# P V groups in any order, a slot for every x row, GpSimd scaling in quarters, the last two softmax blocks scaled on chip: one change to a fused attention and ReGLU kernel

## The chip, the cores and the metric

The kernel runs on one core of a Trainium2 chip. The metric is the device time in microseconds (us). The time before was given as 798.48 us, median of three runs. Every experiment was run beside the kernel before on the same chip; those runs of the kernel before lie between 796.4 and 802.4 us. Medians of different calls therefore differ by up to 1.8 us for the same kernel; the ratios are free of that. All profiles used here were at a mean granted TensorE clock of 0.987 to 1.0. PE is TensorE, ACT is ScalarE, DVE is VectorE, POOL is GpSimd, SP is the engine that issues transfers.

## The reference

2048 rows of width 512 in bf16, 32 heads of 16, hidden width 1792.

```python
xn = layernorm(x)
q, k, v = split(xn @ wqkv)                       # 32 heads of 16
p = softmax(q @ k.T / 4);  o = p @ v             # per head, 2048 keys
h = relu(xn @ W_gate) * (xn @ W_up)
return x + o @ wo + h @ W_down
```

## The kernel before

The kernel is written as a graph of operations. A list scheduler in Python, with an assumed length and latency for each operation, puts them into one queue per engine, and each queue runs in order on the chip. An operation with `lock=True` is kept apart, in the scheduler's own clock, from locked operations of the other engine of the pair GpSimd and DVE. Constants steer it.

```python
PV_LAG = 4.0; D_TAIL = 4; D_LEAD = 10.0; K_ACT = (1, 2)
O_LAST = 66; O_BEG = 22; EV = -940.0; PACE_L = 1.0; KEEP = 4.0; RIDE = 40.0
LAT = {"PE": 150.0, "ACT": 220.0, "DVE": 100.0, "POOL": 120.0, "SP": 0.0}
```

The scores of a unit (128 keys by 512 queries of one head) are computed on PE into PSUM. ACT exponentiates most of them into a ring of six slots; 98 groups of four are exponentiated on DVE by bit operations (four passes out of PSUM, then four long instructions in SBUF, the last two with two inputs). PE multiplies the exponentials by V ("P V"), accumulating in one PSUM bank; column 16 of V is ones, so the row sums come with it. PE fills its spare time with the GLU and with matmuls on zeros.

The parts that the change touches (cuts marked):

```python
# 1 the ones of v_aug: after the fourth row's normalisation in program order only
G.op("POOL", 2500, lambda e: e.memset(v_aug[:, :, :, DH:VN], 1.0), ..., order=t_xn0)
# 2 16 row blocks of x share two slots of four
P_x = Pool("x", 2);  t_x = [Tile("x", P_x) for _ in range(NB)]
# 3 a finished block: sums to DRAM, reciprocal on GpSimd, broadcast back, then one scaling
G.op("POOL", 1280, lambda e: e.tensor_tensor(oT_of(tn), o_sb[:, to.slot, :], rb[:, trb.slot, :], ALU.mult), ..., lock=True)
# 4 P V writes its bank strictly in the order of the units
G.op("PE", 225, pv, mode="col", reads=rd, writes=[pv_tile[key]], prio=u + PV_LAG, ...)
# 5 the very last block on chip: 16 columns of sums, reciprocal, spread by matmuls, product
ins = e.matmul(ps_b[:, 2, 4 * c:4 * c + 4], src(128 * c, 128 * c + 128), ident32[:, DH:128:32], ...)
G.op("DVE", 200, lambda e: e.reciprocal(rrec2[:], ps_b[:, 2, 0:16]), ...)
...  # spread: 16 matmuls of rrec2 columns against the identity; then one product of 128x512
```

The softmax here doesn't subtract the row's maximum and nothing guards it: scores larger than these inputs give would overflow.

Of the kernel before, what the change touches and what calls it, by code (L numbers as in the profile page):

```python
# [6 lines left out]
FP32 = mybir.dt.float32  # L7
# [4 lines left out]
ALU = mybir.AluOpType  # L12
# [16 lines left out]
NRING = 6  # L29
PV_LAG = 4.0  # L30
PV_MIN = 2
# [5 lines left out]
D_SKIP = 14  # L37
D_TAIL = 4
D_LEAD = 10.0
D_WAIT = 1.0  # L40

XT_ACT = ((1,), ())
K_ACT = (1, 2)
V_ACT = (0, 1, 2, 4)
N_POOL = ()
HX = 4
O_END = 70
O_LAST = 66
O_BEG = 22
EV = -940.0  # L50
PACE_L = 1.0

# [33 lines left out]
class Graph:  # L86
# [4 lines left out]
    SWITCH = 100.0  # L91
    KEEP = 4.0
    RIDE = 40.0
    WINDOW = 3400.0
# [51 lines left out]
    def run(self):  # L146
# [111 lines left out]
        self.held = {"DVE": 0.0, "POOL": 0.0}  # L258
        total = len(ops)
        while n < total:  # L260
            best = None
            for e in self.ENGS:
                pick = None
                for o in cand[e]:
                    at = earliest(o)
                    if at is None:
                        continue
                    same = o.mode is not None and o.mode == mode[e]
                    ready = free[e] + (0.0 if same or o.mode is None or mode[e] is None else self.SWITCH)
                    at = max(at, ready)  # L270
                    if o.lock:
                        at = max(at, self.held["POOL" if e == "DVE" else "DVE"])
                    late = at > ready + 1e-6
                    key = (late, at if late else 0.0, o.prio - (self.KEEP if same else 0.0), o.idx)
                    if pick is None or key < pick[0]:
                        pick = (key, at, o)
                if pick is not None and (best is None or pick[1] < best[0]):
                    best = (pick[1], e, pick[2])
            if best is None:
                raise AssertionError("no operation can be placed: %s" % [  # L280
                    (o.name, o.eng) for e in self.ENGS for o in cand[e]][:12])
            at, e, o = best
            if e == "PE":
                if self.fill is not None:
                    blanks(at, o)
                ran.append((at, at + o.dur))
# [125 lines left out]
def bass_parallel_sum__mha_block__glu_gated_reglu__prompt_kernel(  # L412
# [16 lines left out]
    with ExitStack() as es:  # L429
# [40 lines left out]
        ident32 = sb("ident32", [128, 128], FP32)  # L470
        rrec2 = sb("rrec2", [128, 16], FP32)
        ps_sc = es.enter_context(nc.psum_tensor("ps_sc", [128, 5, 512], FP32))
# [15 lines left out]
        P_oT = Pool("oT", 9)  # L488
        P_x = Pool("x", 2)
        P_xr = Pool("xr", 2)  # L490
# [42 lines left out]
        for i in range(2):  # L533
            dma(lambda e, i=i: e.dma_start(q_scr[i, :, DH:2 * DH, :], qT[:, 0, :]), 128,
                reads=[t_qt0], writes=[t_qz[i]], prio=-600)
        t_x = [Tile("x", P_x) for _ in range(NB)]
        t_xm = [Tile() for _ in range(NT)]

        def xs(m):
            return x_sb[:, 4 * t_x[m // 4].slot + m % 4, :]  # L540

        def load_x(m0, n, prio):
            t = t_x[m0 // 4]
            dma(lambda e: e.dma_start(x_sb[:, 4 * t.slot + m0 % 4:4 * t.slot + m0 % 4 + n, :], x_src[:, m0:m0 + n, :]), 128 * n,
                writes=([t] if m0 % 4 == 0 else []), prio=prio)
            o = G.ops[-1]
            if m0 % 4:
                t.r.append(o)
                o.order.add(t.w[0])
            for m in range(m0, m0 + n):  # L550
                t_xm[m].w.append(o)
# [14 lines left out]
        load_x(8, 4, -894)  # L566
        load_x(12, 4, -893)
        dma(lambda e: e.dma_start(Wk[:, :, 128:512], w_src[:, :, D + 128:2 * D]), 384, writes=t_wk[1:], prio=-892)
# [282 lines left out]
        ln_block(0, -800)  # L851
        G.op("POOL", 2500, lambda e: e.memset(v_aug[:, :, :, DH:VN], 1.0), writes=[t_vones], prio=-500, order=t_xn0)
        proj_q(0, 0, -790, tile=t_pro[0], sub=1, eng="ACT")
# [14 lines left out]
        guard = Tile("x")  # L868
        for t in t_x[2:]:
            guard.r.extend(t.w + t.r)  # L870
        P_oT.cur[0:8] = [guard] * 8

        def oT_of(t):
# [127 lines left out]
        t_os, o_last = {}, [[], []]  # L1001

        def last_normalise(to, pr):
            def src(a=0, b=512):
                return o_sb[:, to.slot, a:b]

            t_s, t_r, t_b = Tile("ls", P_b, [2]), Tile(), Tile("lb", P_sc, [1])

            def sums(e):
                ins = None  # L1010
                for c in range(4):
                    ins = e.matmul(ps_b[:, 2, 4 * c:4 * c + 4], src(128 * c, 128 * c + 128), ident32[:, DH:128:32], start=True, stop=True)
                return ins
            o = G.op("PE", 900, sums, mode="full", reads=[to, t_id32], writes=[t_s], prio=pr - 100)
            o.opens = ("tail", [o])
            G.op("DVE", 200, lambda e: e.reciprocal(rrec2[:], ps_b[:, 2, 0:16]), reads=[t_s], writes=[t_r], prio=pr - 900)

            def spread(e):
                ins = None
                for c in range(4):  # L1020
                    for j in range(4):
                        ins = e.matmul(ps_sc[32 * j:32 * j + 32, 3, 128 * c:128 * c + 128],
                                       rrec2[:, 4 * c + j:4 * c + j + 1].to_broadcast([128, 32]), ident32[:],
                                       start=True, stop=True, tile_position=(0, 32 * j))
                return ins
            G.op("PE", 900, spread, mode="col", reads=[t_r, t_id32], writes=[t_b], prio=pr - 100).opens = ()
            tn = Tile("oT", P_oT)
            G.op("DVE", 610, lambda e: e.tensor_tensor(oT_of(tn), ps_sc[:, 3, :], src(), ALU.mult),
                 reads=[t_b, to], writes=[tn], prio=pr - 900)
            return tn  # L1030

        def normalise(c4, gg, ee):
# [3 lines left out]
            to = Tile("o", P_o)  # L1036
            G.op("DVE", 610, lambda e: e.tensor_copy(o_sb[:, to.slot, :], ps_b[:, 0, :]), reads=[tp], writes=[to], prio=-950, name="oev%d" % n)  # L1037
            pr = upos(c4, gg, ee, NT) + 1
            if (c4, gg, ee) == (NB - 1, NGG - 1, 1):
                t_oT[(c4, NGG + ee)] = last_normalise(to, pr)  # L1040
                return
            ts, trr, tsc, trb = Tile("rs"), Tile("rr"), Tile("sc"), Tile("rb", P_rb)
            par = n % 2
            if n >= 2:
# [10 lines left out]
            tn = Tile("oT", P_oT)  # L1055
            G.op("POOL", 1280, lambda e: e.tensor_tensor(oT_of(tn), o_sb[:, to.slot, :], rb[:, trb.slot, :], ALU.mult),  # L1056
                 reads=[to, trb], writes=[tn], prio=pr, lock=True)
            if (c4, gg) == (NB - 1, NGG - 1):
                t_oT[(c4, NGG + ee)] = tn
                return  # L1060
            par = gg % 2
# [12 lines left out]
        def pv_group(key, kt, u):  # L1074
# [12 lines left out]
            for k in range(3 if on else 1):  # L1087
                def pv(e, k=k):
                    ins = None
                    for j in range(4):  # L1090
# [3 lines left out]
                    return ins  # L1094
                G.op("PE", 225, pv, mode="col", reads=rd, writes=[pv_tile[key]], prio=u + PV_LAG, name="pv%d" % u,
                     after=u + PV_MIN)
                if first and k == 0:
                    G.ops[-1].opens = ("pv", [G.ops[-1]])
# [90 lines left out]

        lead = None  # L1190
        for i in range(4):
            tz = Tile("fin", P_sc if i == 0 else P_b if i == 3 else None, [0] if i == 0 else [1])
            if i < 3:
                tz.bank = i
            n0 = len(G.ops)
            m = 12 + i
            if i >= 2:
                G.op("PE", 900, lambda e, i=i, tz=tz: e.matmul(bank_of(tz), ident32[:], resid(i), start=True, stop=False),
                     mode="full", reads=[t_id32, t_res[m]], writes=[tz], prio=NU - 20 if i == 3 else NU + 2)
            for g, pr in ((2, NU - 10), (4, NU - 9), (5, NU + 10)):  # L1200
                to = t_oT[(3, g)]

                def fn(e, i=i, g=g, to=to, tz=tz):
                    ins = None
                    for j in range(4):
                        ins = e.matmul(bank_of(tz)[32 * j:32 * j + 32, :], oT_of(to)[:, 128 * i + 32 * j:128 * i + 32 * j + 32],
                                       Wo[:, g, :] if g < NGG else Wo_p[:, g - NGG, :],
                                       start=(g == 2 and i < 2), stop=(g == 5), tile_position=(0, 32 * j))
                    return ins
                G.op("PE", 216, fn, mode="col", reads=[to, t_wo, t_wop], writes=[tz], prio=pr + (i if g == 5 else 0.1 * i if i < 3 else -9))  # L1210
            mm = [o for o in G.ops[n0:] if o.eng == "PE"]
            if lead is None:
                lead = mm[0]
            elif i < 3:
                for o in mm:
                    o.order.add(lead)
            to_ = Tile("ost", P_xn)
            if i < 2:
                G.op("DVE", 610, lambda e, i=i, to_=to_, tz=tz: e.tensor_tensor(xn_sb[:, to_.slot, :], bank_of(tz), resid(i), ALU.add),
# [55 lines left out]
```

## Time and profile before

| stretch of the kernel before | us |
|---|---|
| start to first exponential | 13.86 |
| first to last exponential | 772.9, of which ACT busy 760.6, idle 12.3 |
| after the last exponential ("tail") | 10.65 |
| span of the profiled run | 797.4 |

### The profile page before, as it was taken

What the parts mean: (1) busy time and instruction counts of PE and PEld (TensorE: products, weight loads), DVE (VectorE), ACT (ScalarE), POOL (GpSimd) and SP (SyncE); (2) the same over time, 40 slices, a digit from 0 to 9 for tenths busy, and PEclk for the clock granted to TensorE, in tenths of its full rate; (3) what the DMA queues carried; (4) which work ended last, traced back from release to release, by engine and by line L of the source; (5) the groups of instructions that cost most, each with busy time, mean ns of one, the idle gap of its engine ahead of it and who ended that gap; (6) DMA issues with size and microseconds to landing.
All of it is one profiled execution on the core that took longest, in us unless ns stands there. A gap on an engine that the chain in (4) does not pass through costs nothing.

```text
span 797.4 us, 21196 instructions
## 1 busy us (share of the span) xinstructions
PE 763.8 (96%) x9386; PEld 226.4 (28%) x9386; DVE 746.9 (94%) x1060; ACT 765.7 (96%) x679; POOL 159.1 (20%) x90
## 2 busy tenths in 40 slices
PE   7999999999999999999999999999999999999997
PEld 3322222222222232222222322222222222222322
DVE  7769999999999999999999999999999999999983
ACT  5899999999999999999999999999999999999995
POOL 3101222211221201223121122121122211122111
PEclk9999999999999999999999999999999999999999
DMA  5132121212121121221222112221222113222001
GB/s 175 50 117 79 34 69 50 55 48 55 49 67 50 28 80 49 68 62 35 61 58 67 35 43 74 58 58 41 73 50 69 41 40 82 62 70 71 21 24 42
DMA packets 96163, 47.10 MB, mean 59 GB/s; under 512 B 70216, under 2 KB 92104, under 8 KB 96072
## 3 DMA queue, kind: packets, MB, share of 16 engines
q1 hardware_dynamic: 96072, 45.74, 21.2%
q8 instruction: 74, 1.21, 0.7%
q14 instruction: 17, 0.14, 0.1%
HBM read 36.96 MB, written 8.51 MB: 57 GB/s over the span
## 4 chain that ended last, share of the span: by engine, by line
DVE 49%; PE 40%; ACT 9%; issue 1%; POOL 0%; DMA 0%; ACTq 0%
DVE dring L1127 16%; PE ps_b L682 15%; PE ps_sc L1111 11%; PE ps_b L1092 9%; ACT ring L1179 9%; DVE dring L1143 8%; DVE dring L1144 8%; DVE dring L1139 4%; DVE dring L1141 4%; PE ps_b L1111 3%; DVE up_sb L898 3%; DVE hT L902 2%; DVE Wv L1037 1%; PE ps_b L1230 1%; DVE qT L737 1%
## 5 line engine op out<-in xcount | busy, mean ns | idle before, releaser
L1179 ACT ACTIVATE ring<-ps_sc 128x1536 bf16<-128x1536 f32 (+1 forms) x663 | 757.3, 1277 | 10.4 <-PE ps_sc L1111 5.6
L1127 DVE TENSOR_SCALAR dring<-ps_b 128x512 uint16<-128x512 f32 x392 | 268.9, 686 | 18.0 <-PE ps_b L1111 15.4
L1111 PE MATMUL ps_sc<-qm,kT 32*128 32x512 bf16 x1656 | 264.2, 385 | 5.9 <-ACT ring L1179 3.7
L1048 POOL TENSOR_TENSOR rrec<-rsum,minus 128x16 f32<-128x16 f32 x31 | 100.9, 3255 | 386.0 <-DMA rsum<-Wv 386.0
L1111 PE MATMUL ps_b<-qm,kT 32*128 32x512 bf16 x392 | 150.0, 383 | 9.7 <-DVE dring L1127 8.3
L1092 PE MATMUL ps_b<-ring,v_aug 128*17 128x512 bf16 x1656 | 149.4, 382 | 1.8 <-DVE Wv L1037 1.7
L1111 PEld LDWEIGHTS ps_sc<-qm,kT 32*128 32x128 bf16 x1656 | 63.4, 91 | 234.2 <-ACT ring L1179 194.6
L1143 DVE TENSOR_TENSOR dring<-dring 128x2048 f16<-128x2048 bf16 x98 | 123.2, 1257 | 0.0
L1144 DVE TENSOR_TENSOR dring<-dring 128x2048 bf16<-128x2048 bf16 x98 | 122.4, 1249 | 0.1
L1056 POOL TENSOR_TENSOR x_sb<-Wv,rb 128x512 bf16<-128x512 f32 x26 | 38.2, 1469 | 175.8 <-DMA rb<-rec_scr 175.8
L1139 DVE TENSOR_SCALAR dring<-dring 128x2048 uint16<-128x2048 uint16 x98 | 69.5, 710 | 1.3
L1141 DVE TENSOR_SCALAR dring<-dring 128x2048 uint16<-128x2048 uint16 x98 | 69.9, 713 | 0.0
L682 PE MATMUL ps_b<-xnT,wgs 128*32 128x512 bf16 x896 | 68.1, 384 | 1.3 <-DVE up_sb L898 1.1
L682 PE MATMUL ps_b<-xnT,wus 128*32 128x512 bf16 x896 | 67.5, 384 | 1.6 <-DVE qT L737 0.6
L1092 PE MATMUL ps_b<-dring,vd 128*17 128x512 bf16 x784 | 66.6, 381 | 0.0
L682 PE MATMUL ps_b<-Wd,hT 128*32 128x512 bf16 x768 | 59.7, 383 | 0.0
L1092 PEld LDWEIGHTS ps_b<-ring,v_aug 128*17 128x17 bf16 x1656 | 37.4, 89 | 65.3 <-issue 45.8
L1111 PEld LDWEIGHTS ps_b<-qm,kT 32*128 32x128 bf16 x392 | 35.6, 91 | 64.3 <-DVE dring L1127 48.3
L1230 PE MATMUL ps_b<-zeros 128*17 128x512 bf16 x560 | 47.4, 382 | 0.0
L1092 PE MATMUL ps_b<-dring,v_aug 128*17 128x512 bf16 x392 | 38.4, 382 | 3.1 <-DVE dring L1144 1.6
L898 DVE COPY up_sb<-ps_b 128x512 f32<-128x512 f32 x56 | 38.3, 684 | 0.8 <-PE ps_b L682 0.7
L902 DVE SCALAR_TENSOR_TENSOR hT<-ps_b,up_sb 128x512 bf16<-128x512 f32 x48 | 32.9, 684 | 0.6 <-PE ps_b L682 0.6
(99 smaller groups left out, 357.8 us busy)
## 6 DMA issues: line engine op xcount, KB each, us to landing
rb<-rec_scr SPq DMA_DIRECT2D x31, 256.0 KB
wus<-in_B_W_up_dram SPq DMA_DIRECT2D x56, 128.0 KB, 3.1
wgs<-in_B_W_gate_dram SPq DMA_DIRECT2D x56, 128.0 KB, 2.4
qm<-q_scr SPq DMA_DIRECT2D x30, 128.0 KB
o_scr<-x_sb SPq DMA_DIRECT2D x25, 128.0 KB
q_scr<-qT SPq DMA_DIRECT2D x17, 128.0 KB
xr_sb<-in_A_x_dram SPq DMA_DIRECT2D x16, 128.0 KB, 3.3
out_dram<-xn_sb SPq DMA_DIRECT2D x16, 128.0 KB, 1.7
```

The lines of the kernel that those rows point to most:

```text
L682: ins = e.matmul(bank_of(tile, sub)[32 * j:32 * j + 32, :], st[:, 32 * j:32 * j + 32], mv, start=(i == 0), stop=(i == n - 1), tile_positio ...
L898: G.op("DVE", 610, lambda e: e.tensor_copy(up_sb[:, tup.slot, :], bank_of(tu)), reads=[tu], writes=[tup], prio=slots[1] + EV)
L1048: G.op("POOL", 3000, lambda e: e.tensor_tensor(rrec[:, par, :], rsum[:, par, :], minus[:, 0:1].to_broadcast([128, 16]), ALU.pow), reads=[t ...
L1092: ins = e.matmul(ps_b[32 * j:32 * j + VN, 0, :], v, src[j][1](k), start=(first and k == 0), stop=(last and (k == 2 or not on)), tile_posit ...
L1111: return e.matmul(bank, kT[32 * j:32 * j + 32, gg, 128 * kt:128 * kt + 128], qm[32 * j:32 * j + 32, t_q[(c4, gg)].slot, ee, :], start=True ...
L1127: o = G.op("DVE", 610, lambda e, j=j: e.tensor_scalar(dring[:, tr.slot, 0, 512 * j:512 * j + 512].bitcast(U16), ps_b[:, 2, :], 0.25 * LOG2 ...
L1139: G.op("DVE", 600, lambda e: e.tensor_scalar(b(2, U16), b(0, U16), 0x7F, 0x3F80, op0=ALU.bitwise_and, op1=ALU.bitwise_or), reads=[tr], wri ...
L1141: G.op("DVE", 600, lambda e: e.tensor_scalar(b(1, U16), b(0, U16), 0xFF80, N_MANT, op0=ALU.bitwise_and, op1=ALU.bitwise_or), reads=[tr], w ...
L1143: G.op("DVE", 1140, lambda e: e.tensor_tensor(b(2, FP16), b(2), b(2), ALU.mult), reads=[tm], writes=[tm], prio=u - 3, name="d4", lock=True)
L1144: G.op("DVE", 1140, lambda e: e.tensor_tensor(b(2), b(0), b(2, FP16), ALU.mult), reads=[tm, tr], writes=[tm], prio=u - 3, name="d5", lock= ...
L1179: return e.activation(ring[:, a:a + n, :], ps_sc[:, 3 * k0:3 * k0 + n, :], ACTF.Exp, scale=0.25)
L1230: ins = e.matmul(ps_b[32 * j:32 * j + VN, 0, :], zeros[:, 0:VN], zmov, start=False, stop=False, tile_position=(0, 32 * j))
```

## The change

Its intent: remove the collisions between GpSimd and DVE, keep ACT fed when a third block of keys is due and when a DVE group is late, and shorten the end.

```diff
-        G.op("POOL", 2500, ...memset..., prio=-500, order=t_xn0)
+        G.op("POOL", 2500, ...memset..., prio=-500, lock=True)      # now waits for the normalisations
+        for o in t_xn0: G.ops[-1].deps[o] = True
-            return x_sb[:, 4 * t_x[m // 4].slot + m % 4, :]
+            return x_sb[:, m, :] if m < 8 else hT[:, m - 8, :]      # a slot for every x row
-            G.op("POOL", 1280, ...tensor_tensor of 128x512...)
+            for k in range(N_MUL): ...  # four of 128x128, name="pm"
+                    if o.name == "pm" ...:  # scheduler: start a quarter with DVE's newest instruction,
+                        ...                 # if that one takes no lock and is long enough
+                if PV_FREE and not (first and k == 0): ...  # P V after the first in any order
-            G.op("DVE", 200, lambda e: e.reciprocal(rrec2[:], ps_b[:, 2, 0:16]), ...)
+            # last block in two halves: sums broadcast to all rows by matmuls, then
+            G.op("DVE", 400, lambda e, h=h, bank=bank: e.reciprocal(rb[..256 columns..], bank()), ...)
+            # the block before it, too, leaves the DRAM trip and is scaled on chip:
+            G.op("DVE", 680, lambda e: e.reciprocal(rb[:, tr.slot, :], ps_b[:, 1, :]), ...)
-PV_LAG = 4.0  D_TAIL = 4  D_LEAD = 10.0  O_LAST = 66  O_BEG = 22  EV = -940.0  PACE_L = 1.0  KEEP = 4.0  RIDE = 40.0
+PV_LAG = 3.0  D_TAIL = 6  D_LEAD = 9.0   O_LAST = 74  O_BEG = 20  EV = -12.0   PACE_L = 0.9  KEEP = 8.0  RIDE = 20.0
...  # K_ACT = (1, 2, 3); the last units' P V given priority; the order of the last output matmuls; one residual added on PE instead of two
```

## The prediction

> **What bounds the kernel now.** I began with the page: busy shares, then the costliest groups.
>
> ```profile
> PE 763.8 (96%) x9386; PEld 226.4 (28%) x9386; DVE 746.9 (94%) x1060; ACT 765.7 (96%) x679; POOL 159.1 (20%) x90
> L1179 ACT ACTIVATE ring<-ps_sc 128x1536 bf16<-128x1536 f32 (+1 forms) x663 | 757.3, 1277 | 10.4 <-PE ps_sc L1111 5.6
> L1230 PE MATMUL ps_b<-zeros 128*17 128x512 bf16 x560 | 47.4, 382 | 0.0
> ```
>
> Three engines look equally full, but PE's 763.8 us hold 47.4 us of matmuls on zeros (blanks that keep it warm), so PE has slack. ACT's 757.3 us of exponentials are real and the change keeps their number. So I read the kernel as "time before the first exponential, plus ACT's work, plus ACT's idle time, plus what follows the last exponential". By windows: the first exponential starts at 13.86 us, the last ends at 786.76, the span is 797.4. Between those two, ACT is busy 760.6 of 772.9 us: 12.3 us idle. A tail of 10.6 us follows. Whatever the change gains must come out of 13.9 + 12.3 + 10.6 us.
>
> Where the 12.3 us lie I took from ACT's timeline (start, duration, engine, line, operation; in brackets the idle time before it and who ended it):
>
> ```profile
> 33.73 0.60 ACT L766 ACTIVATE kT<-ps_b 128x512 bf16<-128x512 f32 x1 [2.84 <-PE ps_b L682]
> 34.82 13.78 ACT L1179 ACTIVATE ring<-ps_sc 128x1536 bf16<-128x1536 f32 x12 [0.49 <-PE ps_sc L1111]
> 49.67 45.53 ACT L1179 ACTIVATE ring<-ps_sc 128x1536 bf16<-128x1536 f32 x40 [1.07 <-PE ps_b L1092]
> ...
> 191.11 146.70 ACT L1179 ACTIVATE ring<-ps_sc 128x1536 bf16<-128x1536 f32 x128 [0.55 <-PE ps_sc L1111]
> ```
>
> Near 34 us ACT is starved for 3.33 us: the third block of keys is late. 1.07 us more is lost at 49.67. After 50 us the idle time comes in 20 gaps of 0.2 to 0.55 us. Setting their times beside GpSimd's scalings (L1056), 18 of them, 5.9 us together, follow a scaling within some 8 us (187.94 before the gap at 191.11, for one). How one becomes the other, in the timeline of all engines:
>
> ```profile
> 353.69 1.42 POOL L1056 TENSOR_TENSOR x_sb<-Wv,rb 128x512 bf16<-128x512 f32 x1 [6.74 <-DMA rb<-rec_scr]
> 353.87 2.31 DVE L1143 TENSOR_TENSOR dring<-dring 128x2048 f16<-128x2048 bf16 x1
> 356.84 0.39 PE L1111 MATMUL ps_b<-qm,kT 32*128 32x512 bf16 x1 [0.86 <-DVE dring L1127]
> 358.20 1.02 ACT L1179 ACTIVATE ring<-ps_sc 128x1024 bf16<-128x1024 f32 x1 [0.40 <-PE ps_sc L1111]
> ```
>
> The VectorE square takes 2.31 us against a median of 1.218; VectorE's PSUM passes then start 1.1 us late; PE, whose queue is in order, waits 0.86 us for the bank; the scores behind it are late and ACT waits 0.40, then 0.33 us.
>
> The start shows the same collision with GpSimd's memset, the fourth row's normalisation taking 2.35 us:
>
> ```profile
> 7.48 2.28 POOL L852 MEMSET v_aug<- 128x512 bf16 x1
> 7.56 2.35 DVE L613 TENSOR_SCALAR xn_sb<-x_sb,mv,rstd 128x512 bf16<-128x512 bf16 x1 [0.46 <-POOL rstd L594]
> ```
>
> And the tail, after the last P V (ends 787.64):
>
> ```profile
> 787.69 0.69 DVE L1037 COPY Wv<-ps_b 128x512 f32<-128x512 f32 x1 [6.86 <-PE ps_b L1092]
> 788.53 0.96 PE L1012 MATMUL ps_b<-ident,Wv 128*128 128x4 f32 x8
> 789.53 0.26 DVE L1016 RECIPROCAL rrec<-ps_b 128x16 f32<-128x16 f32 x1 [1.15 <-PE ps_b L1012]
> 789.86 1.06 PE L1022 MATMUL ps_sc<-ident,rrec 128*32 128x128 f32 x32
> 790.99 0.69 DVE L1028 TENSOR_TENSOR x_sb<-ps_sc,Wv 128x512 bf16<-128x512 f32 x1 [1.20 <-PE ps_sc L1022]
> 793.11 0.59 ACT L1222 ACTIVATE xn_sb<-ps_b 128x512 bf16<-128x512 f32 x1
> ```
>
> A serial ladder: the last eviction ends at 793.70, and the last output transfer, issued at 794.3, lands at 797.4.
>
> **What the Trainium skill says.** "SBUF — State Buffer", section "Who interferes with whom": VectorE in a 2-port mode, or with two SBUF inputs against a GpSimd instruction that reads SBUF, contends with GpSimd, and the later one blocks; one SBUF input outside the 2-port modes does not contend. The trace agrees: L1143 reaches 2.31 us, L1141 1.52, while all 392 PSUM passes L1127 lie between 674 and 698 ns. "PSUM — Partial Sum Buffer", "The four PSUM rules": the first matmul of a group clears the bank's bits, the others accumulate; so any order after the first is right. No number here tests that. "VectorE: DVE Perf Modes", "First, the fixed hardware budget": the reciprocal is an iterative divide "with a repeat count of 8". It gives no time; the only reciprocal here, 128x16, took 257 ns. This is my largest doubt.
>
> **The change part by part.** The instruction orders of both kernels tell what the scheduler did.
>
> *Memset after the fourth row.* It still stands there in GpSimd's queue, but now waits for the normalisations. The fourth takes its alone-time, about 0.56 (the group's mean, 564 ns) instead of 2.35 us, and everything to the first exponential hangs on it: **-1.8 us**.
>
> *A slot for every x row.* Rows 8 to 15 load into hT right after Wv instead of waiting for slots of rows 0 to 7 (issued at 9.94 and 17.92 us). In VectorE's order their statistics move up by five to ten places, and the keys' third and fourth blocks are both evicted by ACT. The 3.33 us starvation should shrink to the step eviction - score - exponential, 0.49 us, while ACT pays 0.6 us for the extra eviction: 3.33 - 0.5 - 0.6, **-2.2 us**. Of the 1.07 us I count half, **-0.5**.
>
> *Scaling in quarters.* 31 instructions of 128x512 (1.27 us alone) become 30 x 4 of 128x128, each started by VectorE's end of the instruction before a PSUM pass. By width a quarter is 0.32 us, perhaps 0.45 with its fixed part; VectorE's passes start 0.60 us apart. It fits, with little to spare. Of the 5.9 us I count 80%: **-4.7 us**. VectorE is freed of its stretches: (1257-1218) x 98 + (1249-1218) x 98 ns = 6.9 us for L1143 and L1144, which is not added, since it acts through these gaps.
>
> *P V in any order.* It lets ready groups pass a group whose VectorE exponential is late. Blanks fall from 560 to 456 matmuls, 104/4 x 0.216 = 5.6 us of PE; PE had slack, so no gain of its own: **0**. It protects the quarters' gain.
>
> *Tail.* Only the last block is on its path. Let E be the end of the last exponential. Before: last P V at E+0.9, last eviction at E+6.9, last issue at E+7.5. After: P V now comes first (E+0.55); copies of 256 columns, 0.35 each (E+0.9); sums broadcast by a matmul, estimated 0.53 for 256 columns from L1022's 1.06 for four sets of 128 (E+1.5, second E+2.05); reciprocals 0.4 each if they run like a copy (E+2.4); products 0.33 each (E+2.75, E+3.05); output matmuls (E+3.5); three adds of 0.6 on VectorE, the fourth eviction on ACT (E+5.1). Last issue E+5.1 instead of E+7.5: **-2.4 us**. Transfers unchanged.
>
> Sum: 1.8 + 2.2 + 0.5 + 4.7 + 2.4 = 11.6, so 798.5 - 11.6 = 786.9 us.
>
> **Rivals.**
> 1. The reciprocal is slow. 257 ns for 16 columns is more than such a size costs otherwise (a 128x128 copy takes 268, so about 150 for 16). If the surplus scales, it is about 7.5 ns a column: 2.0 us for each half, 3.9 us for the 128x512 one. The tail then ends at about E+8.4, 1 us worse than before instead of 2.4 better; and the full-width one, standing before the last VectorE exponential's final product, could hold PE and ACT for a microsecond. Time: 790 to 792. I give it one in three.
> 2. Quarters don't hit the passes: semaphore delay pushes them into the following two-input instruction, four small collisions for one large. Then the gaps stay: 791 to 792. Against: the order is tied by a semaphore to the preceding VectorE instruction.
> 3. ACT isn't the bound and the freed VectorE or PE time moves the end further. Against it: 757 us of exponentials cannot shrink. Floor: first exponential 12.1 + ACT's 760.6 + 0.6 + tail 8.2 = 781.5, with no gap at all.
> 4. Later scalings (four passes instead of one) delay the output rows, with the O_BEG start moved from 22 to 20: PE waits for an o_scr transfer. Each would cost about a microsecond; the DMA trip has slack in most blocks.
>
> **Range and chances.** 786.9, plus 1/3 x 4 for rival 1, gives 788.2, less what I may have undercounted: 788.0. Range 784.5 (all works, nearly no gaps) to 792.5 (rivals 1 or 2, partly). Faster by over 2% means below 782.5, about a microsecond above the floor: 4%. Slower by over 2%: 1%.
>
> **What would show it.** First exponential near 12.1 us; the fourth normalisation near 0.56 us. No gap of 2.8 us before a key eviction on ACT. GpSimd's quarters below 0.5 us, L1143 and L1144 with means near 1220 ns, ACT's idle time between 50 us and the last exponential near 3 us instead of 7.9. The 128x256 reciprocals: 0.4 or 2 us decides the tail, 8.2 or 11.6 us. I am wrong if ACT's idle time stays though the collisions go: then PE's order, not GpSimd, made the gaps.

## The result, and the profile after

The changed kernel took **789.49 us** (median of 4 runs, 788.83 to 791.81) beside 799.51 us for the kernel before; ratio 0.9881, 95% interval 0.9839 to 0.9924. Here and below a ratio is the mean of one kernel's fast runs over the mean of the other's fast runs of the same rounds, so not quite the ratio of the medians. The predicted 788.0 is 1.5 us below it, and the range held it.

First the page of the changed kernel, engines and costly groups (busy us and mean ns of one; then the idle time before them):

```profile
PE 756.7 (96%) x9270; PEld 225.2 (29%) x9270; DVE 740.0 (94%) x1065; ACT 763.3 (97%) x679; POOL 165.0 (21%) x178
...
L1232 ACT ACTIVATE ring<-ps_sc 128x1536 bf16<-128x1536 f32 (+1 forms) x663 | 755.2, 1279 | 6.6 <-PE ps_sc L1164 4.9
L1197 DVE TENSOR_TENSOR dring<-dring 128x2048 bf16<-128x2048 bf16 x98 | 119.5, 1219 | 0.0
L1196 DVE TENSOR_TENSOR dring<-dring 128x2048 f16<-128x2048 bf16 x98 | 119.4, 1219 | 0.0
L1104 POOL TENSOR_TENSOR x_sb<-Wv,rb 128x128 bf16<-128x128 f32 x100 | 46.3, 465 | 285.3 <-DVE dring L1197 77.7
```

The two long DVE products (L1143 and L1144 before, L1197 and L1196 now) have a mean of 1219 ns where it had been 1257 and 1249; the longest of either now is 1277 ns, and it was 2.31 us before. The quarters (L1104) take 465 ns on average. In the trace 115 of the 120 miss the two products or overlap one by less than 0.04 us. Five meet one for longer: three start inside a product (at 68, 69 and 653 us) and are themselves long (807, 1457 and 1181 ns), while the product keeps its 1216 to 1219 ns; one reaches 0.20 us into the product of 1277 ns, and one leaves no mark.

ACT's timeline after has only three gaps of 0.15 us or more between the first and last exponential, where the kernel before had 23:

```profile
11.37 2.37 ACT L1232 ACTIVATE ring<-ps_sc 128x1536 bf16<-128x1536 f32 x2 [0.58 <-PE ps_sc L1164]
...
29.56 5.97 ACT L1232 ACTIVATE ring<-ps_sc 128x1536 bf16<-128x1536 f32 x5 [0.59 <-PE ps_sc L1164]
...
484.52 282.48 ACT L1232 ACTIVATE ring<-ps_sc 128x1536 bf16<-128x1536 f32 x248 [0.44 <-PE ps_b L1164]
770.71 5.36 ACT L1232 ACTIVATE ring<-ps_sc 128x1536 bf16<-128x1536 f32 x5 [3.72 <-PE ps_sc L1164]
```

The start comes 2.49 us sooner and the starvation near 30 us is 0.59 instead of 3.33 us. But a gap of 3.72 us stands near the end, where there was none. The timeline of all engines shows how it comes about:

```profile
764.82 3.35 DVE L1080 RECIPROCAL rb<-ps_b 128x512 f32<-128x512 f32 x1
...
768.23 0.62 PE L1262 MATMUL ps_b<-Wo,x_sb 128*32 128x512 bf16 x4 [2.65 <-DVE rb L1080]
...
770.06 0.61 PE L1164 MATMUL ps_sc<-qm,kT 32*128 32x512 bf16 x3
```

The 128x512 reciprocal holds DVE and its PSUM bank for 3.35 us. PE's in-order queue has, next, an output matmul into that bank, waits 2.65 us for it, and the scores behind it (770.06) come late for ACT. The tail has two more reciprocals in a row:

```profile
777.91 0.64 PE L1036 MATMUL ps_b<-Wv,ident 128*32 128x256 f32 x8
...
778.62 1.76 DVE L1042 RECIPROCAL rb<-ps_b 128x256 f32<-128x256 f32 x1 [0.68 <-PE ps_b L1036]
...
780.30 1.69 DVE L1042 RECIPROCAL rb<-ps_sc 128x256 f32<-128x256 f32 x1
...
781.91 0.69 DVE L1047 TENSOR_TENSOR x_sb<-rb,Wv 128x256 bf16<-128x256 f32 x2
```

The books, from the windows of both profiled runs (us):

| term | before | after | difference | predicted |
|---|---|---|---|---|
| start to first exponential | 13.86 | 11.37 | -2.49 | -1.8 |
| ACT idle, first exponential to 60 us | 4.41 | 0.72 | -3.69 | -3.3 (2.8 + 0.5) |
| ACT idle, 60 to 740 us | 6.97 | 1.35 | -5.62 | -4.7 |
| ACT idle, 740 us to last exponential | 0.88 | 3.91 | +3.03 | 0 |
| ACT busy between first and last | 760.6 | 758.7 | -1.9 | +0.6 |
| tail | 10.65 | 12.03 | +1.38 | -2.4 |
| sum | | | -9.3 | -11.6 |

ACT's busy time fell although it evicts one block of keys more. By shape, the 331 exponentials of 128x1536 (mean 1490 ns) and the 331 of 128x1024 (1070 ns) sum to 847.4 us, but the group is busy for only 755.2 us: consecutive ones overlap by 92.2 / 662 = 0.14 us. If a gap also costs the overlap that it interrupts, twenty gaps fewer are worth an estimated 20 x 0.14 = 2.8 us, less 0.6 for the eviction, which is near the 1.9 measured. That this is the cause is not shown: the runs e10 and e4 below have 13 and 12 gaps of 0.15 us or more where the changed kernel has three, with the same evictions, and ACT is busy for 758.2 and 758.4 us in them, not longer than the 758.7 here.

### The profile page after: what moved, and what is told of

The parts are those of the page before. It is cut to its first block, busy times and chain, and to the rows that moved or that the text cites.

```text
span 788.1 us, 21088 instructions
## 1 busy us (share of the span) xinstructions
PE 756.7 (96%) x9270; PEld 225.2 (29%) x9270; DVE 740.0 (94%) x1065; ACT 763.3 (97%) x679; POOL 165.0 (21%) x178
## 4 chain that ended last, share of the span: by engine, by line
DVE 46%; PE 26%; ACT 26%; issue 1%; DVEq 0%
ACT ring L1232 25%; DVE dring L1180 16%; PE ps_b L697 10%; DVE dring L1196 8%; PE ps_sc L1164 7%; DVE dring L1197 6%; PE ps_b L1140 5%; DVE dring L1192 4%; DVE dring L1194 4%; DVE up_sb L916 3%; DVE hT L920 2%; PE ps_b L1164 2%; DVE Wv L1068 1%; PE ps_b L863 1%; DVE xn_sb L958 1%
## 5 line engine op out<-in xcount | busy, mean ns | idle before, releaser
L1232 ACT ACTIVATE ring<-ps_sc 128x1536 bf16<-128x1536 f32 (+1 forms) x663 | 755.2, 1279 | 6.6 <-PE ps_sc L1164 4.9
L1164 PE MATMUL ps_sc<-qm,kT 32*128 32x512 bf16 x1656 | 264.7, 385 | 6.6 <-ACT ring L1232 4.1
L1164 PE MATMUL ps_b<-qm,kT 32*128 32x512 bf16 x392 | 150.1, 383 | 8.8 <-DVE dring L1180 6.3
L1140 PE MATMUL ps_b<-ring,v_aug 128*17 128x512 bf16 x1656 | 152.1, 384 | 0.3 <-DVE Wv L1068 0.2
L1094 POOL TENSOR_TENSOR rrec<-rsum,minus 128x16 f32<-128x16 f32 x30 | 96.3, 3211 | 228.6 <-DMA rsum<-Wv 228.6
L1164 PEld LDWEIGHTS ps_sc<-qm,kT 32*128 32x128 bf16 x1656 | 63.4, 91 | 231.5 <-ACT ring L1232 202.3
L1197 DVE TENSOR_TENSOR dring<-dring 128x2048 bf16<-128x2048 bf16 x98 | 119.5, 1219 | 0.0
L1196 DVE TENSOR_TENSOR dring<-dring 128x2048 f16<-128x2048 bf16 x98 | 119.4, 1219 | 0.0
L1104 POOL TENSOR_TENSOR x_sb<-Wv,rb 128x128 bf16<-128x128 f32 x100 | 46.3, 465 | 285.3 <-DVE dring L1197 77.7
L1192 DVE TENSOR_SCALAR dring<-dring 128x2048 uint16<-128x2048 uint16 x98 | 67.9, 693 | 1.7
L1194 DVE TENSOR_SCALAR dring<-dring 128x2048 uint16<-128x2048 uint16 x98 | 67.6, 689 | 0.0
L697 PE MATMUL ps_b<-xnT,wgs 128*32 128x512 bf16 x896 | 66.2, 383 | 1.3 <-DVE up_sb L916 1.0
L1140 PE MATMUL ps_b<-dring,vd 128*17 128x512 bf16 x784 | 65.5, 381 | 0.0
L1140 PEld LDWEIGHTS ps_b<-ring,v_aug 128*17 128x17 bf16 x1656 | 38.5, 89 | 65.3 <-issue 46.7
L1164 PEld LDWEIGHTS ps_b<-qm,kT 32*128 32x128 bf16 x392 | 35.6, 91 | 66.0 <-DVE dring L1180 52.9
L1140 PE MATMUL ps_b<-dring,v_aug 128*17 128x512 bf16 x392 | 38.6, 384 | 1.5 <-DVE dring L1197 0.7
L1282 PE MATMUL ps_b<-zeros 128*17 128x512 bf16 x456 | 38.9, 382 | 0.0
```

What stands on the lines that cost most here:

```text
L697: ins = e.matmul(bank_of(tile, sub)[32 * j:32 * j + 32, :], st[:, 32 * j:32 * j + 32], mv, start=(i == 0), stop=(i == n - 1), tile_positio ...
L1094: G.op("POOL", 3000, lambda e: e.tensor_tensor(rrec[:, par, :], rsum[:, par, :], minus[:, 0:1].to_broadcast([128, 16]), ALU.pow), reads=[t ...
L1140: ins = e.matmul(ps_b[32 * j:32 * j + VN, 0, :], v, src[j][1](k), start=(first and k == 0), stop=(last and (k == 2 or not on)), tile_posit ...
L1164: return e.matmul(bank, kT[32 * j:32 * j + 32, gg, 128 * kt:128 * kt + 128], qm[32 * j:32 * j + 32, t_q[(c4, gg)].slot, ee, :], start=True ...
L1192: G.op("DVE", 600, lambda e: e.tensor_scalar(b(2, U16), b(0, U16), 0x7F, 0x3F80, op0=ALU.bitwise_and, op1=ALU.bitwise_or), reads=[tr], wri ...
L1194: G.op("DVE", 600, lambda e: e.tensor_scalar(b(1, U16), b(0, U16), 0xFF80, N_MANT, op0=ALU.bitwise_and, op1=ALU.bitwise_or), reads=[tr], w ...
```

## The experiments

The theory after the result: (a) the removed collisions and the starvation give what the table shows; (b) the long reciprocals take back some 4 us, by the gap and in the tail. Rivals: the tuning constants, not the parts, made the gain; DVE's lateness, not PE's order, made the gap; and, from the third group of runs on, that all parts are smaller than what a different schedule does by itself.

**Short reciprocals (e1).** The changed kernel with both on-chip blocks done as the kernel before did its last one: sums into 16 columns, a reciprocal of 128x16, a spread by matmuls.

```diff
-  G.op("DVE", 680, lambda e: e.reciprocal(rb[:, tr.slot, :], ps_b[:, 1, :]), ...)
+  G.op("DVE", 200, lambda e: e.reciprocal(rrec2[:, 16:32], ps_b[:, 1, 0:16]), ...)
-  # two halves: G.op("DVE", 400, lambda ...: e.reciprocal(rb[.. 256 columns ..], bank()), ...)
+  G.op("DVE", 200, lambda e: e.reciprocal(rrec2[:, 0:16], ps_b[:, 2, 0:16]), ...)
+  # + 16 matmuls each that spread rrec2; products read PSUM
```

> The changed kernel with the three wide reciprocals (128x512: 3.35 us, 128x256: 1.76 and 1.69 us) replaced, for both of the last two softmax blocks, by the way of the kernel before for the last one: sums gathered into 16 columns, a 128x16 reciprocal (0.26 us), a broadcast by matmuls (1.06 us). Theory (the wide reciprocal stands in VectorE's queue, PE's queue waits for the bank and ACT starves): ACT's gap of 3.72 us near 770 us goes altogether, the tail after the last exponential falls from 12.0 to about 10.5 us, the whole to 784.3 us (5.2 us under the changed kernel). Rival (PE's order near the end makes the gap, whatever stands in VectorE's queue): the gap stays above 2 us and only the tail's 1.5 us are won, about 788.

Measured: **785.56 us** (785.28 to 786.19), ratio 0.9833 (0.981 to 0.9857), faster than both kernels. The first line below is the reciprocal of the block before last, the last one that of the last block; the line between is ACT, in the timeline near the end:

```profile
764.31 0.26 DVE L1082 RECIPROCAL rrec<-ps_b 128x16 f32<-128x16 f32 x1
...
764.64 8.29 ACT L1244 ACTIVATE ring<-ps_sc 128x1024 bf16<-128x1024 f32 x8 [0.21 <-PE ps_sc L1176]
...
775.96 0.26 DVE L1038 RECIPROCAL rrec<-ps_b 128x16 f32<-128x16 f32 x1 [1.15 <-PE ps_b L1034]
```

ACT's idle time after 740 us fell from 3.91 to 0.27 us and the tail from 12.03 to 11.07, not to the 10.5 expected. TensorE's queue differs from the changed kernel's in 24 lines (counted as for the table below), so this is the same schedule with shorter reciprocals. (b) holds, the tail in part; e12 looks at what is left of it.

**True lengths told to the scheduler (e2).** The reciprocals stay; only the scheduler's idea of their length is mended.

```diff
-  G.op("DVE", 400, ...reciprocal of 128x256...)
+  G.op("DVE", 1690, ...)
-  G.op("DVE", 680, ...reciprocal of 128x512...)
+  G.op("DVE", 3280, ...)
```

> The changed kernel with only the scheduler's idea of the long reciprocals' lengths corrected (680 to 3280 ns for 512 columns, 400 to 1690 ns for each half); the instructions are the same, VectorE's, ScalarE's and GpSimd's queues too, and only TensorE's order near the end differs: the Wo matmul into the bank that the reciprocal holds, and the P V of the late VectorE group, move behind scores. If the 3.72 us gap of the changed kernel comes from TensorE's in-order queue standing behind the reciprocal's bank, the gap falls under 1 us, the time falls by about 3 us to 786.5, and the tail stays at 12.0 us, since the two short reciprocals are still in it. If VectorE itself being late makes the gap (its groups hold the ring of exponentials, whatever the order of TensorE), the gap stays over 2 us and the time is 789.5.

Measured: **786.71 us** (786.54 to 787.04), ratio 0.9849 (0.983 to 0.9867). Only 19 lines of TensorE's queue differ, and no other queue's order does. The reciprocal is as long as it was; scores (L1164) now stand between it and the output matmul (L1262), and ACT has no gap to its last exponential:

```profile
758.62 14.27 ACT L1232 ACTIVATE ring<-ps_sc 128x1536 bf16<-128x1536 f32 x13
...
765.67 3.35 DVE L1080 RECIPROCAL rb<-ps_b 128x512 f32<-128x512 f32 x1
...
767.99 0.39 PE L1164 MATMUL ps_sc<-qm,kT 32*128 32x512 bf16 x2
...
769.08 0.40 PE L1262 MATMUL ps_b<-Wo,x_sb 128*32 128x512 bf16 x4 [0.16 <-DVE rb L1080]
```

So the gap came from PE's order behind a mis-stated length, not from DVE being late: the rival fell. (The edit moved two things on PE behind scores, the output matmul and the P V of the late DVE group; in the changed kernel's timeline it is the output matmul that waits, for 2.65 us.) The tail stayed (12.31 us), as it should with the two half reciprocals still in it.

**The memset's wait undone (e5).**

```diff
-  G.op("POOL", 2500, ...memset..., prio=-500, lock=True);  for o in t_xn0: G.ops[-1].deps[o] = True
+  G.op("POOL", 2500, ...memset..., prio=-500, order=t_xn0)
```

> The changed kernel with GpSimd's memset of v_aug again free to run beside the fourth row's normalisation. Theory (the two collide, and the first exponential waits): the fourth normalisation takes 2.3 us again instead of 0.4, the first exponential starts 1.8 to 2.5 us later, near 13.5 us, and the whole is 2 to 2.5 us slower, 791.5 to 792. Rival (the earlier start is eaten up near 29 us, where the keys are waited for anyway): start later, but the time within 0.8 us of 789.5.

Measured: 792.77 us, ratio 0.9941 (0.9926 to 0.9955), 3.3 us slower than the changed kernel where 2 to 2.5 was expected. PE's and DVE's queues are in the changed kernel's order. The fourth normalisation and the memset, in the timelines of the start, first the changed kernel, then this one:

```profile
7.71 0.41 DVE L628 TENSOR_SCALAR xn_sb<-x_sb,mv,rstd 128x512 bf16<-128x512 bf16 x1 [0.46 <-POOL rstd L609]
...
8.18 2.37 POOL L867 MEMSET v_aug<- 128x512 bf16 x1 [0.51 <-DVE xn_sb L628]
```

```profile
7.44 2.30 POOL L867 MEMSET v_aug<- 128x512 bf16 x1
7.52 2.36 DVE L628 TENSOR_SCALAR xn_sb<-x_sb,mv,rstd 128x512 bf16<-128x512 bf16 x1 [0.46 <-POOL rstd L609]
...
12.96 2.37 ACT L1230 ACTIVATE ring<-ps_sc 128x1536 bf16<-128x1536 f32 x2 [0.58 <-PE ps_sc L1162]
```

The collision is back, and with it 1.59 us of the start (12.96 against 11.37). Most of the rest is ACT's idle time: 5.02 us after 740 us instead of 3.91, in the same order of queues.

**One scaling instead of four (e3), and only the quarters in the kernel before (e7).**

```diff
 e3, from the changed kernel
-N_MUL = 4
+N_MUL = 1      # and neither the name "pm" nor its rule
 e7, from the kernel before
-  G.op("POOL", 1280, ...tensor_tensor of 128x512...)
+  for k in range(4): G.op("POOL", 470, ...columns 128 * k to 128 * k + 128..., name="pm")
+  # and the scheduler's rule for "pm"
```

> The changed kernel with GpSimd's scaling as one 128x512 instruction again, bound to no VectorE pass; everything else as changed. Theory (collisions made the small gaps): L1196 and L1197 stretch again to means of 1245 ns or more, some 15 gaps of ACT come back between 50 and 760 us, 5 us or more of idle time against 1.5, the whole 5 to 7 us slower, 795. Rival (the free P V order and the new priorities closed the gaps): ACT's idle time there stays under 2.5 us and the time within 1.5 us of 789.5.

> The kernel before with only the quarters: the four 128x128 scalings and the rule that places them in VectorE's PSUM passes; nothing else of the change. Theory (the quarters alone close the gaps): ACT's idle time between 50 and 766 us falls from 7.6 to about 2 us, the square and product to means of 1220 ns, the time from 799.5 to about 793, while the start (13.9 us), the 3.3 us of starvation near 34 us and the tail of 10.6 us stay. Rival (it takes the free order as well): less than 3 us won, 797 or more.

Measured: e3 807.52 us (ratio 1.0099, 1.0064 to 1.0135), 18 us slower than the changed kernel; e7 793.13 us (ratio 0.9925, 0.9898 to 0.9952), the expected 6 us gain. But its terms are not those expected: ACT's idle time between 50 and 766 us fell from 7.6 to 4.1 us, not to 2; the start came 0.7 us sooner (13.18) though nothing in it was changed, ACT's busy time fell by 2.6 us, and the tail grew by 0.7. In e3 the collision is as before: a scaling of 1.27 us, a product of 2.22 us instead of 1.22, an ACT gap of 1.22 us four microseconds on:

```profile
589.51 1.27 POOL L1104 TENSOR_TENSOR x_sb<-Wv,rb 128x512 bf16<-128x512 f32 x1 [8.72 <-DMA rb<-rec_scr]
589.64 2.22 DVE L1197 TENSOR_TENSOR dring<-dring 128x2048 bf16<-128x2048 bf16 x1
...
593.52 1.02 ACT L1232 ACTIVATE ring<-ps_sc 128x1024 bf16<-128x1024 f32 x1 [1.22 <-PE ps_sc L1164]
```

ACT's idle time from 60 to 740 us is 10.44 us (1.35 in the changed kernel), but 10.97 us more lie after 740, and nothing in the expectation covers those (it had 5 to 7 us in all). I first read them as the price of the collisions. The two nudged runs below forbid that reading.

**The order of P V fixed again (e4).**

```diff
-PV_FREE = 1
+PV_FREE = 0
```

> The changed kernel with P V groups summed in their fixed order again, everything else as changed. My prediction gave the free order nothing of its own: within 1.5 us of 789.5, ACT's idle time between 50 and 760 us under 3 us. Rival (the order freed PE from waiting for late VectorE groups and so closed the gaps): PE waits again for VectorE's last product before P V, ACT idles 5 us or more there, 793 to 796.

Measured: 802.06 us (ratio 1.004, 1.0012 to 1.0068), 12.6 us slower, with 9.48 us of ACT idle from 60 to 740 and 8.24 after. My own expectation fell, and the rival's 793 to 796 us was passed by 6 us too.

**The x slots shared again (e6).**

```diff
-            return x_sb[:, m, :] if m < 8 else hT[:, m - 8, :]
+            return x_sb[:, 4 * t_x[m // 4].slot + m % 4, :]
+        P_x = Pool("x", 2)      # and the loads and guards that go with it
```

> The changed kernel with only eight slots for x rows again, so that rows 8 to 15 wait for the slots of rows 0 to 7. Theory: ACT starves again for 2 to 3.5 us before the third block of keys, and the whole is 2 to 3 us slower, 791.5 to 792.5. Rival (the third key eviction on ACT and the new order, not the slots, closed that gap): the gap near 29 us stays under 1 us, time within 0.8 us of 789.5.

Measured: 799.76 us (ratio 1.0032, 1.0004 to 1.0061), 10 us slower where 2 to 3 was expected. The expected piece is there, a key eviction that waits:

```profile
31.40 0.60 ACT L784 ACTIVATE kT<-ps_b 128x512 bf16<-128x512 f32 x1 [3.39 <-PE ps_b L700]
```

ACT's idle time before 60 us is 4.13 instead of 0.72. But 9.09 us are lost after 740, where no x row plays a part.

**The old constants, with P V free (e9) and fixed (e8).** The changed code with the nine constants of the kernel before. With these the scheduler found no place for the sum of the block before last in bank 1, so both have it in bank 2.

```diff
-PV_LAG = 3.0 ... RIDE = 20.0     # the nine lines of the change
+PV_LAG = 4.0 ... RIDE = 40.0
-PV_FREE = 1
+PV_FREE = 0                      # e8 only
```

> The changed kernel with the scheduler's nine retuned numbers (P V lag, VectorE lead and tail, the times of the output rows, the priority of evictions, the mode constants) set back to those before; free P V order, quarters, slots and on-chip scaling stay; the sum of the last block but one goes to another PSUM bank, since it cannot be placed otherwise. Theory (free order and quarters do the work, the retuning little): within 2 us of 789.5, ACT's idle time between 50 and 750 us under 3.5 us. Rival (the retuning is worth several us): 793 or more.

> As the run with the old tuning, and P V in its fixed order too. Theory (the fixed order cost 12.6 us only together with the new tuning, which lets P V fall behind the output rows until the ring of exponentials is full): about 790 to 793, as the kernel before with quarters alone suggests (793.1, less 5 us of start and keys, plus 4 to 5 us of wide reciprocals), and no gap of ACT over 1.2 us that ends with a P V matmul except near the wide reciprocal. Rival (the fixed order by itself costs 10 us or more with the other parts of the change): 799 or more, with gaps of ACT of 1 to 3 us ended by P V matmuls.

Measured: e9 794.40 us (ratio 0.9961, 0.9946 to 0.9976); e8 798.69 us (1.0012, 0.9996 to 1.0027). Both theories missed: e9 landed where its rival said (793 or more), and e8 is 6 us over its own range, 0.3 us short of its rival's. The free order is worth 4.3 us here and 12.6 with the new constants: a part whose worth triples with the constants isn't measured by either pair.

**Two meaningless nudges (e10, e11).** One latency that the scheduler assumes is moved by 5 ns. None of the work changes; which instruction comes next does, and with it the number of filler matmuls on zeros (456 in the changed kernel, 528 and 580 here).

```diff
-    LAT = {"PE": 150.0, ..., "DVE": 100.0, ...}
+    LAT = {"PE": 155.0, ..., "DVE": 100.0, ...}      # e10
+    LAT = {"PE": 150.0, ..., "DVE": 105.0, ...}      # e11
```

> The changed kernel with one assumption of the scheduler moved that means nothing on the chip (TensorE's latency 150 to 155 ns): the same work in another order of TensorE's queue. It measures how far the time depends on which schedule comes out. If luck of the schedule is a large part of what the other runs showed beyond their expected sizes (one scaling +18, x slots +10), the time differs from 789.5 by 2 to 6 us, with the difference in ScalarE's gaps near the end. If those runs showed effects of their own parts, it is within 1 us of 789.5.

> As the run with TensorE's latency moved, but with VectorE's assumed latency, 100 to 105 ns: a second draw of the schedule. If luck of the schedule matters, 2 to 6 us from 789.5 in either direction; if not, within 1 us. In either case the first exponential should stay at 11.0 to 11.4 us, and no gap over 1 us should stand before the middle.

Measured: e10 **797.63 us** (796.76 to 798.17, ratio 0.9984, 0.9964 to 1.0004), e11 **799.61 us** (798.72 to 799.89, ratio 1.0011, 0.9989 to 1.0033). A nudge costs 8.1 and 10.1 us, more than I had allowed for (2 to 6): the whole gain of the change. The first exponentials are at 11.20 and 11.04 us, as expected; gaps over 1 us before the middle, which I had ruled out, are there (1.28 us at 164, 1.77 us at 389). The timeline of e10 near the end shows what a poorer order does:

```profile
755.25 1.91 PE L697 MATMUL ps_b<-Wd,hT 128*32 128x512 bf16 x32
...
756.99 0.60 PE L697 MATMUL ps_b<-Wo,x_sb 128*32 128x512 bf16 x8
...
757.42 0.39 PE L1140 MATMUL ps_b<-dring,vd 128*17 128x512 bf16 x4
...
757.63 1.04 PE L1140 MATMUL ps_b<-ring,v_aug 128*17 128x512 bf16 x16
...
758.07 2.37 ACT L1232 ACTIVATE ring<-ps_sc 128x1024 bf16<-128x1024 f32 x2 [3.54 <-PE ps_b L1140]
```

PE has 40 output matmuls (Wd, Wo) ahead of 20 P V matmuls. No slot of the ring comes free until those P V run, and ACT stands for 3.54 us. The releaser (P V, L1140) says that ACT waited for a ring slot; gaps after L1164 are waits for scores. After 740 us two of e10's gaps (6.8 us) and three of e11's (6.9 us) are of the ring kind. With the P V order free they occur all the same: free order allows a good schedule but doesn't make one.

**The tail's residual matmuls after the last P V (e12).** In e1 they stood before the last P V. Edit to e1:

```diff
   # the four matmuls that add the residual of one output block, in the tail
+  G.ops[-1].order.add(pv_tile[(NB - 1, NGG - 1, 1)].w[-1])
```

> The version with both 16-column reciprocals, with the matmuls that add the residual in the tail ordered after the last P V matmuls on TensorE. If they stand in the way of the last P V, the tail falls from 11.07 to about 10.7 us and the time from 785.56 to about 785.2 us. If TensorE isn't what the tail waits for there, nothing changes in it, and the different order of TensorE elsewhere moves the time by 1 us either way.

Measured: **784.42 us** (784.22 to 784.68), ratio 0.982 (0.9802 to 0.9838), the fastest version. Its first copy after P V starts 0.50 us after the last exponential's end (1.12 in e1), and the tail is 10.26 us, 0.81 less, where 0.4 was expected. Against e1 this is a comparison across two chips, whose medians of the kernel before differ by 0.46 us; the tail inside the profiles is what I rely on. TensorE's queue differs from e1's in 8 lines. The last P V and the first copy, e1's first; L1266 is a residual matmul:

```profile
773.19 0.49 PE L1266 MATMUL ps_sc<-xnT,ident 128*128 128x128 f32 x2
773.61 0.40 PE L1152 MATMUL ps_b<-ring,v_aug 128*17 128x512 bf16 x4
774.05 0.76 DVE L1064 COPY Wv<-ps_b 128x256 f32<-128x256 f32 x2 [6.54 <-PE ps_b L1152]
```

```profile
772.94 0.76 DVE L1064 COPY Wv<-ps_b 128x256 f32<-128x256 f32 x2 [5.92 <-PE ps_b L1152]
```

All kernels side by side. "Rows moved" counts the lines in which `diff` finds TensorE's queue, as the scheduler builds it with one line for each operation, to differ from that of the changed kernel (some 5,700 if nothing agreed); idle is ACT's, in us.

| kernel | rows moved | idle first-60 | idle 60-740 | idle 740-last | tail | median us | ratio |
|---|---|---|---|---|---|---|---|
| before | 2783 | 4.41 | 6.97 | 0.88 | 10.65 | 799.51 | |
| changed | 0 | 0.72 | 1.35 | 3.91 | 12.03 | 789.49 | 0.9881 |
| e5 memset | 0 | 0.71 | 1.95 | 5.02 | 11.86 | 792.77 | 0.9941 |
| e2 true lengths | 19 | 0.72 | 2.23 | 0.06 | 12.31 | 786.71 | 0.9849 |
| e1 short reciprocals | 24 | 0.71 | 2.25 | 0.27 | 11.07 | 785.56 | 0.9833 |
| e12 e1 + P V first | 28 | 0.72 | 1.73 | 0.28 | 10.26 | 784.42 | 0.9820 |
| e10 nudge PE | 2372 | 1.16 | 3.91 | 8.83 | 12.23 | 797.63 | 0.9984 |
| e11 nudge DVE | 2279 | 0.76 | 4.40 | 10.20 | 11.95 | 799.61 | 1.0011 |
| e6 x slots | 2146 | 4.13 | 3.17 | 9.09 | 12.11 | 799.76 | 1.0032 |
| e3 one scaling | 2150 | 0.72 | 10.44 | 10.97 | 11.52 | 807.52 | 1.0099 |
| e4 P V fixed | 2420 | 0.72 | 9.48 | 8.24 | 11.88 | 802.06 | 1.0040 |
| e9 old constants | 2695 | 1.52 | 4.03 | 3.80 | 12.30 | 794.40 | 0.9961 |
| e8 old, P V fixed | 2791 | 1.52 | 8.37 | 4.59 | 11.76 | 798.69 | 1.0012 |
| e7 quarters only | 2786 | 4.40 | 3.34 | 1.48 | 11.34 | 793.13 | 0.9925 |

The table splits the runs into two kinds. The five rows from "changed" to e12 share one schedule, and their differences are those of the edits, but for some scatter: from 60 to 740 us, where their queues agree, their idle time lies between 1.35 and 2.25 us. The rest are redrawn schedules: their totals carry the scatter of 8 to 10 us that the nudges show. In those only a stretch can be read, and only against the nudges in the same stretch. So read: one scaling leaves 10.4 us of idle from 60 to 740, the nudges 3.9 and 4.4, hence about 6 us for the quarters, which is what e3 had been expected to cost (5 to 7); in e7 the idle time of that stretch fell by 3.6 us (6.97 to 3.34). Since e4 and e8 idle for 9.5 and 8.4 us there with the quarters in place, the sum alone doesn't prove it. The places do: of ACT's gaps of 0.15 us or more in this stretch, 16 of 17 in the kernel before (5.4 us) and 18 of 23 in e3 (8.0 us) end within 8 us after a scaling starts, but only 2 of 7 in e10 (0.4 us), 3 of 6 in e11 (0.8 us) and 3 of 8 in e7 (0.9 us). Shared x slots leave 4.13 us before 60, the nudges 1.16 and 0.76, hence about 3 us (2 to 3 expected). The 8 to 11 us after 740 in e3, e4 and e6 are about as large as in the nudged kernels (8.8 and 10.2), so they can't be credited to a part.

One thing I had overlooked: the scheduler itself foresees much of this. Its own end time, read by building the kernels without running them, is 784.3 us for the changed kernel and 793.0 and 794.2 for e10 and e11, that is 8.7 and 9.8 us more, where 8.1 and 10.1 were measured. (It does not foresee collisions: e3 has 790.4 by the scheduler and took 807.52.)

## Why the prediction was right, and where it was not

**Memset: right.** 1.8 us predicted, 2.49 found at the start, of which e5 gives back 1.59 when the wait alone is undone. The start of one profiled run is uncertain by some 0.7 us: e7 has the queues of the kernel before up to there and starts at 13.18 instead of 13.86. The fourth normalisation alone took 0.41 us, not the group's mean of 0.56. The Trainium skill's "SBUF — State Buffer", section "Who interferes with whom", says that a VectorE instruction in a 2-port mode and a GpSimd instruction lock each other out for a whole instruction: 2.36 against 0.41 us in these two runs agree.

**A slot for every x row: right.** 3.33 us fell to 0.59; e6 brings back 3.39 us before the eviction.

**Quarters: right.** Idle time from 60 to 740 us fell by 5.62 (predicted 4.7), or by 4.7 to 5.6 over the five kernels of this schedule; the two products' mean is 1219 ns (near 1220 predicted), a quarter 465 ns (0.45 predicted). Rival 2, quarters that slip into the next product, came true for five of the 120 and left no gap of ACT behind: the longest product is 1277 ns.

**ACT's busy time: a missing term.** I counted the added eviction (0.6 us) and nothing else, but ACT's busy time fell by 1.9 us. Overlap regained where gaps closed, 0.14 us each, is a possible cause, which e10 and e4 don't bear out; it stays open. (Rival 3's floor of 781.5 us took this time as fixed, too.)

**The tail: two wrong steps.** "Reciprocals 0.4 each if they run like a copy" failed: 1.76 and 1.69 us for 256 columns, 3.35 us for 512. Rival 1 was the right account, with 6.5 ns a column (3.35 us / 512) instead of its 7.5 (its own figures, (257 - 150) / 16, make 6.7). It foresaw the last issue at E+8.4 us, which came at E+8.9, and a hold of "a microsecond" by the full-width one; the runs show a tail 1.38 us longer than before and a gap of 3.72 us. e2 and e1 show both sizes: ending the gap alone gives 2.8 us (789.49 to 786.71), short reciprocals 3.9 us (to 785.56; the medians come from different calls, with 799.51, 798.68 and 799.14 us for the kernel before). I had given this rival one chance in three and counted 1.3 us for it; in the books the end cost 4.4 us (3.03 + 1.38) where my sum had a gain of 2.4. The other step is "P V now comes first (E+0.55)": residual matmuls stood between the last P V, the first copy began at E+1.12 (before: E+0.94) and the first reciprocal at E+2.55, where my ladder had it at E+1.5. e12 takes this delay away and wins 0.81 us of the tail. Even with both mended, by the longer way over 16 columns, its tail is 10.26 us, 0.4 under the kernel before's and not 2.4.

**P V in any order: neither right nor wrong by these runs.** I put it at 0. With the order fixed, idle time from 60 to 740 us is 9.5 (e4) and 8.4 us (e8), against 3.9 to 4.4 in the nudged kernels and 4.0 in e9; but e7, whose order is fixed too, has 3.3. Some 4 to 5 us where the other parts are present is my estimate from these numbers; it is not shown.

**Why the total fitted.** The start and the middle gained 13.7 us (2.49 + 3.69 + 5.62 + 1.9) where I had 9.2 (1.8 + 3.3 + 4.7 - 0.6); the end lost 4.4 where I had a gain of 2.4. The two misses mostly cancel. And both my numbers and the measured ones belong to one schedule of the changed kernel. My working read its queues, so it did predict that schedule, but nothing in it said that a neighbour, 5 ns of assumed latency away, has no gain at all. The range of 8 us that I gave is narrower than the scatter between schedules. How far the kernel before would move under the same nudge was not run, so whether its 799 us is a lucky or a usual draw stays open, and with it what the change is worth on average. The scheduler's own end times give a hint, not run on the chip: with TensorE's latency at 145, 155 and 160 ns, DVE's at 95, 105 and 110, or ACT's at 215 and 225, one at a time, the changed kernel goes from 784.3 us to 787.8 to 794.7 (mean 791.2), the kernel before from 789.0 to 788.9 to 795.9 (mean 792.0). So both kernels as built are good draws, the changed one the best of its nine. What is shown is the worth of the parts in their stretches.

## What to carry to other kernels

When a scheduler places the instructions, run the changed kernel once or twice with a nudge that means nothing, and read the scheduler's own end time, before crediting a total to a part; then compare parts only inside one schedule, or stretch by stretch against the nudged runs. Measure an operation at the size in which you will use it and tell the scheduler that length: here lengths told too short (680 ns for some 3300, 400 for some 1700) cost 2.8 us, and a 16-column reciprocal did the work of a 512-column one. When a time fits a prediction, check the books term by term, since two errors can cancel.

## What the Trainium skill lacked or had wrong

- "VectorE: DVE Perf Modes", section "First, the fixed hardware budget", names the reciprocal's repeat count of 8 but gives no time. The runs show 3.35 us for 128x512 fp32, 1.76 and 1.69 us for 128x256 and 0.26 us for 128x16: 6.5 to 6.9 ns a column for the wide ones.
- "ScalarE: Activation LUTs", section "What ACT_TABLE_LOAD costs", gives 186 ns + 0.833 ns a column for an ACTIVATE with immediates, and an overlap of consecutive ones of about 93 ns. Durations are near it (1490 ns for 1536 columns, where it makes 1466; 1070 for 1024, where it makes 1039), but the overlap here is 0.14 us.
- No page says that two builds of one kernel which differ only in the order of their queues and in their filler matmuls can be 8 to 10 us (1.0 to 1.3%) apart, as the two nudged runs are from the changed kernel.
